# The attention output product: one head at a time over 64 partitions, in two PSUM banks, in place of head pairs with a zero-padded matrix

## The chip, the core and the metric

The program runs on one core of one Trainium2 chip. The metric is device time in microseconds, from the launch to the last write. The engines are TensorE (PE, with its weight loads shown apart as PEld), VectorE (DVE), ScalarE (ACT), GpSimd (POOL) and SyncE (SP), which here only issues transfers. SBUF and PSUM have 128 partitions; PSUM has 8 banks of 512 fp32 values per partition. A matmul holds one operand in the array (the stationary one, loaded beforehand, at most 128 partitions by 128 columns) and streams the other one past it; the columns of the stationary operand become the partitions of the result.

## The reference, cut to what matters

```python
# q, k, v: (4 batches, 8 heads, 576 tokens, 64)
kv  = einsum('bhsd,bhse->bhde', k, v)          # a 64 x 64 matrix for each batch and head
out = einsum('bhsd,bhde->bhse', q, kv)         # the "o product"
rms = sqrt(mean(out * out, axis=-1) + 1e-6)    # for each token and head
x   = out / rms * g_norm                       # then (b, s, h*d): 2304 tokens x 512
h = x @ w_in                                   # 512 -> 1024
solu = h * softmax(h); ln = layernorm(solu) * g_ln
x2 = ln @ w_out                                # 1024 -> 512
result = ((x2 @ w_a) * (x2 @ w_b)) @ w_out2    # 512 -> 1536 -> 512
```

The change touches `kv` and `out` alone. The weights arrive as 64-bit floats and are narrowed on the chip.

## The kernel before, in words

**Tiles.** The 2304 tokens are 18 tiles of 128. A batch has 576 tokens, four full tiles and 64 left over; the leftovers of two batches share a tile, so tiles 8 and 17 are mixed: 64 tokens of one batch, 64 of the next. The other 16 are full.

**Two parts.** The first part runs from the start to some 300 us and takes each tile through attention, the first feed-forward layer up to the layer norm, and (two tiles at a time) `w_out`. The second part, the last product and the two that are multiplied, is not touched.

**The steps of a tile**, by the tokens that the written order uses for them, with the engine that does the work:

- `kp` (PE, `kv_product`, L334) makes the two 64 x 64 matrices of one batch and one pair of heads, the even head on partitions 0 to 63 of a PSUM tile, the odd head on 64 to 127. `kk` (DVE) or `ka` (ACT), both `kv_keep` (L347), copy them into `kvb`, in two instructions.
- `qt` (PE, L358) transposes a tile of q, all heads: of each pair of heads, the even one lands on partitions 0 to 63 and the odd one on 64 to 127. `qk` (ACT) copies that to `qT`.
- `op` (PE, `o_product`, L370) multiplies. `kvb` for a head pair is a 128 x 128 matrix with the even head's 64 x 64 block top left, the odd head's bottom right and zeros elsewhere, so one matmul over 128 partitions gives both heads. The stationary operand is `qT` of the pair (128 partitions by 128 tokens), and the 128 columns of `kvb` stream. A full tile takes 4 such matmuls, a mixed tile 8 with 64 tokens each. The operands are plain fp32, and each matmul stands as two instructions in the trace. The result of all heads is one PSUM bank, `po`.
- `os` (ACT, `o_square`, L385) squares `po`, `om` (DVE, then POOL) sums the squares per head and takes the reciprocal root in ten small POOL instructions, `ox` (DVE, `o_scale`, L400) multiplies `po` by it. `ox` is the last reader of `po`.
- `xt`, `xh`, `xl` transpose the scaled tile (PE) and split it into a high and a low part (ACT, DVE); `hp` (PE) is the product with `w_in`, 24 matmuls into two banks of its own; `hm`, `he`, `hs`, `hq`, `hn` are maximum, exponential, product, squares and norm on DVE, ACT and POOL; `lt0`, `lt1`, `lh0` to `ll1` transpose and split the result; `yp` (PE) and `yk` (ACT) are a quarter of the product with `w_out` for two tiles and its copy.

**Order.** Each engine works strictly in the order in which the program names its instructions. That order is written out by hand: `PROLOGUE` (L26) until the tile before slot 5, then the strings `SLOT` (L37, tiles up to slot 9) and `LATER` (L41) once for each tile. A token with `+2` works on the tile two ahead. B, M, E and their like narrow weights in between on ACT, DVE and POOL. In the slots `op` stands between `xt` and `yp` (`SLOT`) or between `xt` and `lt0` (`LATER`), and `ox` near the very end. The prologue has seven `op`, the slots eleven.

**PSUM.** `hp` has two banks of its own. All other results of PE in this part take one bank each out of the pool `ps_t` (L175), six banks; a bank comes free when the last reader of its tile in the written order is done, and a product that finds none free waits.

Of the kernel before, what the change touches and what calls it, by code (L numbers as in the profile page):

```python
# [8 lines left out]
F32 = mybir.dt.float32  # L9
# [4 lines left out]
AF = mybir.ActivationFunctionType  # L14
ALU = mybir.AluOpType
# [4 lines left out]
P = 128  # L20
# [80 lines left out]
def tile_attention_moe(ctx, tc, q, k, v, g_norm, w_in, w_out, g_ln, w_a, w_b, w_out2, out):  # L101
    nc = tc.nc
    B, H, S, D = q.shape
# [3 lines left out]
    NP = H // 2  # L107
# [19 lines left out]
    tiles = []  # L127
# [19 lines left out]
    def pool(name, bufs, stack=left, side="left", **kw):  # L147
        if side == "right":
            kw["side"] = "right"
        if stack is psum:  # L150
            kw["space"] = PSUM
        return stack.enter_context(tc.tile_pool(name=name, bufs=bufs, **kw))
# [11 lines left out]
    wt = pool("wt", 1, top)  # L164
# [10 lines left out]
    ps_t = pool("ps_t", 6, psum)  # L175
# [6 lines left out]

    const.tile([P, 80], F32, name="lpad")

    kvb = [wt.tile([P, NP, P], F32, name=f"kvb{n}") for n in range(3)]
    for t in kvb:
        nc.gpsimd.memset(t, 0.0)

    def rsqrt(v, n, tag, eng=nc.gpsimd):

# [110 lines left out]
    qT = {}  # L301
# [45 lines left out]
    def kv_keep(copy=nc.vector.tensor_copy):  # L347
        if kvps:
            b, hp, pk = kvps.pop(0)
            for n in range(2):  # L350
                ns = slice(n * D, (n + 1) * D)
                copy(kvb[b % 3][ns, hp, ns], pk[ns])
            ready.add((b, hp))

    ready = set()
    psum_of = {}
# [12 lines left out]

    def o_product(i):  # L370
        assert all((b, hp) in ready for b, _, _ in tiles[i] for hp in range(NP))
        po = ps_t.tile([P, NP, P], F32, tag="t", name="po").rearrange("p n (two d) -> p (n two) d", two=2)
        for hp in range(NP):
            a = 0
            for b, _, n in tiles[i]:
                nc.tensor.matmul(  # L376
                    po[a:a + n, 2 * hp:2 * hp + 2, :], qT[i][:, hp, a:a + n], kvb[b % 3][:, hp, :],
                    start=True, stop=True,
                )
                a += n  # L380
        psum_of["o", i] = po

    sqs = {}

    def o_square(i):  # L385
        sqs[i] = tx.tile([P, H, D], F32, tag="sq", name="sq", bufs=1)
        nc.scalar.activation(sqs[i], psum_of["o", i], AF.Square)

    rms = {}

# [9 lines left out]
    def o_scale(i):  # L400
        x = tx.tile([P, H, D], F32, tag="x", name="x")
        r = rms.pop(i).rearrange("p (h o) -> p h o", o=1).to_broadcast([P, H, D])
        nc.vector.tensor_tensor(out=x, in0=psum_of.pop(("o", i)), in1=r, op=ALU.mult)
        xt[i] = x.rearrange("p h d -> p (h d)")


# [582 lines left out]
    def load_gl(_):  # L989
# [5 lines left out]
        B=lambda _: begin(), BP=lambda _: begin(True), M=lambda _: mid(), MM=lambda _: mid(2),  # L995
        E=lambda _: end(), EV=lambda _: end(nc.vector),
        kp=kv_product, kk=lambda _: kv_keep(), ka=lambda _: kv_keep(nc.scalar.copy),
        qt=q_turn, qk=q_keep, op=o_product, os=o_square, om=o_rms, ox=o_scale, xt=x_turn, xh=x_hi, xl=x_lo,
        hp=h_product, hm=h_max, he=h_exp, hs=h_solu, hq=h_square, hn=h_norm,
        lt0=lambda i: l_turn(i, 0), lt1=lambda i: l_turn(i, 1),  # L1000
# [46 lines left out]
    i = NTILE - 2  # L1047
# [8 lines left out]
    i = NTILE - 1  # L1056
# [30 lines left out]
    t = p2["x2"].tile([P, 14 * TB + 3 * LINE], F32R, tag="x", name="x2")  # L1087
    t = t[:, :14 * TB].rearrange("p (h n c t) -> p h n c t", h=2, n=7, c=2)
# [5 lines left out]
    for n, (count, which) in enumerate(((1, now), (6, later), (5, now), (2, later))):  # L1094
# [3 lines left out]
        for _ in range(count):  # L1098
            part, n = which.pop(0)
# [18 lines left out]
    for j in range(1, NJ - 1):  # L1118
        n = 2 * j + 2
# [181 lines left out]
```

## Time and profile before

| what | value |
|---|---|
| median of 2 runs | 701.88 us (701.71 to 702.06) |
| the profiled execution's own time | 702.19 us |
| its span on the core | 700.1 us |
| PE, PEld busy | 665.7 us (95%), 633.0 us (90%) |
| DVE, ACT, POOL busy | 519.6 us (74%), 284.1 us (41%), 302.8 us (43%) |
| mean granted TensorE clock | 0.995 of full speed |

The profile is one execution, recorded by the hardware. A group of instructions is named by its line, its engine and what it writes and reads: `po<-kvb,qT` is the o product, `kvp<-vs,ks` the kv product, `sq<-po` the square, `x<-po,y_a` the scaling, `xtp`, `ltp`, `qtp` the three kinds of transposes, `ph<-wih,xh` and the like the product with `w_in`, `x2p` that with `w_out`. Matmuls overlap: the recorded duration of one is its time through the array, while the next one starts earlier, so the rate is read from starts. A row of several merged instructions gives the first start and the time to the last end. Clock 1.00 is full speed.

### The profile page before, as it was taken

What the parts mean: (1) busy time and instruction counts of PE and PEld (TensorE: products, weight loads), DVE (VectorE), ACT (ScalarE), POOL (GpSimd) and SP (SyncE); (2) the same over time, 40 slices, a digit from 0 to 9 for tenths busy, and PEclk for the clock granted to TensorE, in tenths of its full rate; (3) what the DMA queues carried; (4) which work ended last, traced back from release to release, by engine and by line L of the source; (5) the groups of instructions that cost most, each with busy time, mean ns of one, the idle gap of its engine ahead of it and who ended that gap; (6) DMA issues with size and microseconds to landing.
All of it is one profiled execution on the core that took longest, in us unless ns stands there. A gap on an engine that the chain in (4) does not pass through costs nothing.

```text
span 700.1 us, 12578 instructions
## 1 busy us (share of the span) xinstructions
PE 665.7 (95%) x4710; PEld 633.0 (90%) x4710; DVE 519.6 (74%) x930; ACT 284.1 (41%) x491; POOL 302.8 (43%) x446
## 2 busy tenths in 40 slices
PE   1699999999999999999999999999999999999998
PEld 1577798999999998899999999999998899999998
DVE  3889977676688776779656867577656779987883
ACT  2558854544455346543331122212212445443431
POOL 2588776677666311113654467444672140000000
PEclk9899999999999999999999999999999999999999
DMA  9998645645542502342344336544334694654521
GB/s 248 316 248 234 184 127 156 168 127 149 178 127 76 167 16 68 106 136 81 111 149 136 118 106 187 177 136 142 112 95 129 221 313 139 190 146 130 150 76 61
DMA packets 107132, 103.84 MB, mean 148 GB/s; under 512 B 25280, under 2 KB 94400, under 8 KB 107072
## 3 DMA queue, kind: packets, MB, share of 16 engines
q1 hardware_dynamic: 101024, 94.40, 46.3%
q10 hardware_dynamic: 6048, 8.65, 3.7%
q8 instruction: 37, 0.61, 0.4%
q14 instruction: 23, 0.19, 0.1%
HBM read 71.05 MB, written 31.98 MB: 147 GB/s over the span
## 4 chain that ended last, share of the span: by engine, by line
PE 76%; DVE 9%; issue 5%; POOL 4%; DMA 3%; ACT 1%; SPq 1%; DVEq 0%; ACTq 0%; POOLq 0%
PE pw L710 26%; PE pq L881 18%; PE x2p L527 5%; PE x2p L525 5%; PE x2p L526 5%; PE ph L438 4%; PE ph L440 4%; PE ph L439 4%; PE ltp L495 2%; PE po L376 2%; DMA vs<-in_v_dram 1%; POOL a L751 1%; DMA wo<-w2d 1%; DMA gw<-gd 1%; PE xtp L413 1%
## 5 line engine op out<-in xcount | busy, mean ns | idle before, releaser
L751 POOL TENSOR_TENSOR a<-b,a 128x384 f32<-128x384 f32 x53 | 63.3, 1208 | 127.2 <-DVE b L740 126.2
L710 PE MATMUL pw<-xh,wh 128*128 128x384 f32 x336 | 114.3, 340 | 2.6 <-DVE b L761 1.6
L710 PE MATMUL pw<-xh,wl 128*128 128x384 f32 x336 | 112.7, 335 | 0.0
L710 PE MATMUL pw<-xl,wh 128*128 128x384 f32 x336 | 112.6, 335 | 0.0
L710 PE MATMUL pw<-x,wh 128*128 128x384 f32 x336 | 85.8, 336 | 0.9 <-DVE b L740 0.6
L525 PE MATMUL x2p<-lh,woh 128*128 128x256 f32 x288 | 82.6, 287 | 0.3 <-ACT lh L505 0.2
L526 PE MATMUL x2p<-ll,woh 128*128 128x256 f32 x288 | 80.6, 280 | 0.8 <-DVE ll L508 0.8
L527 PE MATMUL x2p<-lh,wol 128*128 128x256 f32 x288 | 80.6, 280 | 0.5 <-DVE wol L50 0.5
L710 PEld LDWEIGHTS pw<-xh,wh 128*128 128x128 f32 x336 | 63.1, 188 | 7.1 <-DVE b L761 2.3
L710 PEld LDWEIGHTS pw<-xl,wh 128*128 128x128 f32 x336 | 63.1, 188 | 0.0
L710 PEld LDWEIGHTS pw<-xh,wl 128*128 128x128 f32 x336 | 63.1, 188 | 0.0
L710 PEld LDWEIGHTS pw<-x,wh 128*128 128x128 f32 x336 | 60.5, 188 | 1.8 <-DVE b L740 0.9
L438 PE MATMUL ph<-wih,xh 128*128 128x512 f32 x144 | 56.9, 395 | 0.8 <-DVE so L461 0.8
L881 PE MATMUL pq<-wo,gh 128*128 128x256 f32 x336 | 57.7, 276 | 0.0
L440 PE MATMUL ph<-wih,xl 128*128 128x512 f32 x144 | 56.3, 391 | 1.2 <-DVE xl L423 1.2
L439 PE MATMUL ph<-wil,xh 128*128 128x512 f32 x144 | 56.3, 391 | 0.4 <-DVE wil L50 0.4
L710 PE MATMUL pw<-x,wl 128*128 128x384 f32 x168 | 56.2, 335 | 0.0
L527 PEld LDWEIGHTS x2p<-lh,wol 128*128 128x128 f32 x288 | 54.6, 190 | 0.9 <-DVE wol L50 0.9
L526 PEld LDWEIGHTS x2p<-ll,woh 128*128 128x128 f32 x288 | 54.2, 188 | 1.2 <-DVE ll L508 1.2
L525 PEld LDWEIGHTS x2p<-lh,woh 128*128 128x128 f32 x288 | 54.2, 188 | 0.9 <-ACT lh L505 0.5
L881 PE MATMUL pq<-wo,gw 128*128 128x256 f32 x450 | 53.1, 276 | 0.0
L67 POOL TENSOR_SCALAR nu<-nu 128x512 f32<-128x512 f32 x23 | 44.7, 1955 | 17.1 <-ACT nu L62 16.1
(158 smaller groups left out, 1536.0 us busy)
## 6 DMA issues: line engine op xcount, KB each, us to landing
gd<-a SPq DMA_DIRECT2D x72, 192.0 KB, 2.0
ring<-in_moe_w_out_dram SPq DMA_DIRECT2D x20, 512.0 KB, 5.4
gl<-gd SPq DMA_DIRECT2D x14, 384.0 KB, 3.5
gw<-gd SPq DMA_DIRECT2D x12, 384.0 KB, 3.2
ring<-in_moe_w_in_dram SPq DMA_DIRECT2D x8, 512.0 KB, 7.3
qs<-in_q_dram SPq DMA_DIRECT2D x16, 256.0 KB, 6.5
x2d<-x2s ACTq DMA_DIRECT2D x32, 128.0 KB, 1.8
st<-in_moe_w_a_dram SPq DMA_DIRECT2D x8, 512.0 KB, 4.3
```

The costliest lines, as they stand in the source:

```text
L67: eng.tensor_scalar(out=u, in0=u, scalar1=2.0 ** -15, scalar2=122879.9921875, op0=ALU.max, op1=ALU.min)
L376: nc.tensor.matmul(po[a:a + n, 2 * hp:2 * hp + 2, :], qT[i][:, hp, a:a + n], kvb[b % 3][:, hp, :], start=True, stop=True,)
L438: nc.tensor.matmul(ph[:, n, :], xh[:, c, :], wh, start=(c == 0), stop=False)
L439: nc.tensor.matmul(ph[:, n, :], xh[:, c, :], wl, start=False, stop=False)
L440: nc.tensor.matmul(ph[:, n, :], xl[:, c, :], wh, start=False, stop=(c == NK - 1))
L495: nc.tensor.transpose(pt[:, m, :], hs_[i]["so"][:, f * P:(f + 1) * P], ident)
L525: nc.tensor.matmul(pa, wh[:, cs], lh[:, f, :], start=(f == 0), stop=False)
L526: nc.tensor.matmul(pa, wh[:, cs], ll[:, f, :], start=False, stop=False)
L527: nc.tensor.matmul(pa, wl[:, cs], lh[:, f, :], start=False, stop=(f == NF1 - 1))
L710: nc.tensor.matmul(out, wt_[:, wn, c], xt_[xn][:, c], start=first and c == n == 0, stop=c == 1 and n == 2, skip_group_check=not first,)
L751: eng.tensor_tensor(out=a[n], in0=by, in1=a[n], op=ALU.mult)
L881: nc.tensor.matmul(ps, xt_[:, c], wt_[:, c], start=first and c == n == 0, stop=c == NJ - 1 and n == 2, skip_group_check=not first,)
```

## The change

`kvb` loses its zeros: it holds 64 columns for each head pair, the even head on partitions 0 to 63 and the odd one on 64 to 127, so the three memsets go and `kv_keep` copies a pair in one instruction. `o_product` issues one matmul for each head, over its 64 partitions: the stationary operand is 64 partitions by 128 tokens (64 in a mixed tile), and 64 columns stream. The even heads' results go to one PSUM bank and the odd heads' to another, head pair by head pair in turn, so a full tile has 8 matmuls in place of 4 and a mixed tile 16 in place of 8, and each takes two banks of `ps_t` and not one. `o_square` and `o_scale` do the two banks one after the other, 256 elements each, and write every second group of 64 of the same tiles as before. The order of the tokens is unchanged.

```diff
@@ -182,9 +182,7 @@
 
     const.tile([P, 80], F32, name="lpad")
 
-    kvb = [wt.tile([P, NP, P], F32, name=f"kvb{n}") for n in range(3)]
-    for t in kvb:
-        nc.gpsimd.memset(t, 0.0)
+    kvb = [wt.tile([P, NP, D], F32, name=f"kvb{n}") for n in range(3)]
 
     def rsqrt(v, n, tag, eng=nc.gpsimd):
 
@@ -347,9 +345,7 @@
     def kv_keep(copy=nc.vector.tensor_copy):
         if kvps:
             b, hp, pk = kvps.pop(0)
-            for n in range(2):
-                ns = slice(n * D, (n + 1) * D)
-                copy(kvb[b % 3][ns, hp, ns], pk[ns])
+            copy(kvb[b % 3][:, hp], pk)
             ready.add((b, hp))
 
     ready = set()
@@ -369,22 +365,28 @@
 
     def o_product(i):
         assert all((b, hp) in ready for b, _, _ in tiles[i] for hp in range(NP))
-        po = ps_t.tile([P, NP, P], F32, tag="t", name="po").rearrange("p n (two d) -> p (n two) d", two=2)
+        po = [ps_t.tile([P, NP, P], F32, tag="t", name=f"po{n}")[:, :, :D] for n in range(2)]
         for hp in range(NP):
             a = 0
-            for b, _, n in tiles[i]:
-                nc.tensor.matmul(
-                    po[a:a + n, 2 * hp:2 * hp + 2, :], qT[i][:, hp, a:a + n], kvb[b % 3][:, hp, :],
-                    start=True, stop=True,
-                )
-                a += n
+            for b, _, rows in tiles[i]:
+                for n in range(2):
+                    ns = slice(n * D, (n + 1) * D)
+                    nc.tensor.matmul(
+                        po[n][a:a + rows, hp, :], qT[i][ns, hp, a:a + rows], kvb[b % 3][ns, hp, :],
+                        start=True, stop=True,
+                    )
+                a += rows
         psum_of["o", i] = po
+
+    def of_head(t, n):
+        return t.rearrange("p (hp two) d -> p hp two d", two=2)[:, :, n]
 
     sqs = {}
 
     def o_square(i):
         sqs[i] = tx.tile([P, H, D], F32, tag="sq", name="sq", bufs=1)
-        nc.scalar.activation(sqs[i], psum_of["o", i], AF.Square)
+        for n, po in enumerate(psum_of["o", i]):
+            nc.scalar.activation(of_head(sqs[i], n), po, AF.Square)
 
     rms = {}
 
@@ -400,7 +402,8 @@
     def o_scale(i):
         x = tx.tile([P, H, D], F32, tag="x", name="x")
         r = rms.pop(i).rearrange("p (h o) -> p h o", o=1).to_broadcast([P, H, D])
-        nc.vector.tensor_tensor(out=x, in0=psum_of.pop(("o", i)), in1=r, op=ALU.mult)
+        for n, po in enumerate(psum_of.pop(("o", i))):
+            nc.vector.tensor_tensor(out=of_head(x, n), in0=po, in1=of_head(r, n), op=ALU.mult)
         xt[i] = x.rearrange("p h d -> p (h d)")
 
 
```

## Rows read from the trace of the kernel before

**Rows 1.** The page: the span, and the chain that ended last by engine

```profile
span 700.1 us, 12578 instructions
...
PE 76%; DVE 9%; issue 5%; POOL 4%; DMA 3%; ACT 1%; SPq 1%; DVEq 0%; ACTq 0%; POOLq 0%
```

**Rows 2.** Stretch 96.2 to 258.6: busy us of PE, PEld, DVE, ACT, POOL; then L376

```profile
96.20:258.60 162.40, 162.09 (x1207) 147.92 (x1206) 119.30 (x261) 75.59 (x144) 99.43 (x192) 1.00 0.48 138
...
96.20:258.60 162.40, 11.70 (x104) 10.45 (x104) 1.00 0.48 138
```

**Rows 3.** PE in order of time, 147.6 to 149.0: start, us, line, shape, count

```profile
147.98 1.06 PE L376 MATMUL po<-kvb,qT 128*128 128x128 f32 x8
```

**Rows 4.** PE in order of time, 118.4 to 119.9, around a mixed tile

```profile
118.21 0.49 PE L413 MATMUL xtp<-ident,x 128*128 128x128 f32 x3
118.63 1.09 PE L376 MATMUL po<-kvb,qT 128*64 128x128 f32 x16
119.66 0.39 PE L525 MATMUL x2p<-lh,woh 128*128 128x256 f32 x1
119.88 0.28 PE L526 MATMUL x2p<-ll,woh 128*128 128x256 f32 x1
```

**Rows 5.** PE in order of time, 151.5 to 152.6, a kv product

```profile
151.71 0.80 PE L342 MATMUL kvp<-vs,ks 128*64 128x64 f32 x20
```

**Rows 6.** Weight loads (PEld) in order of time, at 24.4 and at 118.6

```profile
24.36 0.30 PEld L376 LDWEIGHTS po<-kvb,qT 128*128 128x128 f32 x2 [1.30 <-ACT qT L367]
...
118.63 0.20 PEld L376 LDWEIGHTS po<-kvb,qT 128*64 128x64 f32 x4 [0.17 <-ACT lh L505]
```

**Rows 7.** Groups by line and shape on ACT: count, busy us, mean ns

```profile
L535 ACT COPY x2s<-x2p 128x256 f32<-128x256 f32 x32 | 12.0, 374 | 20.0 <-PE x2p L527 16.9 <-ACT x2s L535 1.8 <-DMA x2d<-x2s 1.1
...
L387 ACT ACTIVATE sq<-po 128x512 f32<-128x512 f32 x18 | 11.0, 610 | 0.8 <-PE po L376 0.7
```

**Rows 8.** Groups by line and shape on DVE

```profile
L740 DVE TENSOR_TENSOR b<-pw,b 128x384 f32<-128x384 f32 x54 | 29.6, 552 | 12.3 <-PE pw L710 12.3
...
L403 DVE TENSOR_TENSOR x<-po,y_a 128x512 f32<-128x512 f32 x18 | 12.4, 688 | 6.1 <-POOL y_a L203 6.0
...
L352 DVE COPY kvb<-kvp 64x64 f32<-64x64 f32 x16 | 3.5, 220 | 0.3
```

**Rows 9.** The chain that ended last, 0 to 97 us: start, us, what

```profile
22.15 0.61 ACT sq L387
...
28.46 0.69 DVE x L403
...
73.95 0.60 DVE x L403
```

**Rows 10.** PE in order of time, 61 to 98, the late prologue

```profile
62.11 1.04 PE L362 MATMUL qtp<-ident,qs 128*128 128x128 f32 x8
63.07 0.80 PE L342 MATMUL kvp<-vs,ks 128*64 128x64 f32 x20
64.56 1.13 PE L376 MATMUL po<-kvb,qT 128*128 128x128 f32 x8 [0.68 <-DVE ll L508]
65.61 0.80 PE L342 MATMUL kvp<-vs,ks 128*64 128x64 f32 x20
66.98 0.47 PE L438 MATMUL ph<-wih,xh 128*128 128x512 f32 x1 [0.56 <-DVE so L461]
...
87.54 0.29 PE L525 MATMUL x2p<-lh,woh 128*128 128x256 f32 x1
```

**Rows 11.** DVE in order of time, 61 to 98

```profile
64.33 0.74 DVE L423 SCALAR_TENSOR_TENSOR xl<-xtp,gn,xh 128x512 fp32r<-128x512 f32 x1
...
67.90 0.68 DVE L508 TENSOR_TENSOR ll<-ltp,lh 128x512 fp32r<-128x512 f32 x1
...
72.73 1.23 DVE L446 TENSOR_REDUCE nm<-ph 128x1 f32<-128x1024 f32 x1
...
89.64 0.69 DVE L403 TENSOR_TENSOR x<-po,y_a 128x512 f32<-128x512 f32 x1 [1.25 <-POOL y_a L203]
```

## Prediction before the change was run

> **What bounds the kernel now.** I read the page first: one core, and PE on 76% of the chain that ended last [rows 1]. The idle time of the other engines is therefore worth little by itself. Then I cut the time into stretches. From 96.2 to 258.6 us, PE is busy in 162.09 of 162.40 us at the full 2.4 GHz clock, and the o product (L376) takes 11.70 of them in 104 instructions [rows 2]: nine tiles of 8 and the two mixed tiles of 16, since one fp32 matmul is two instructions on PE. In that stretch each nanosecond that the o product gains or loses on PE goes to the end. Before it, up to 96 us, the seven other o products lie in the written-out prologue, where the chain runs mostly over DVE and POOL; there the question is what PE is kept waiting for. After 258.6 us nothing of the change runs.
>
> **Term 1, the o product on PE.** A full tile now issues 8 instructions; the last starts 1.06 - 0.275 us (one instruction) after the first, so the step is 0.112 us and the block 0.895 us [rows 3]. The change issues 16 instructions: each streams 64 columns and not 128, over 64 partitions, with 128 tokens still stationary. So streaming halves per instruction and the number of instructions doubles. The gain depends on two neighbours on different row halves of the array running side by side, and on the weight loads.
>
> *Streaming.* The trace has neighbours on different column halves: 20 instructions of 64 columns with 64 stationary columns last 0.80 us with the final 0.22, so a pair of them takes 0.058 us [rows 5], and they do run in pairs. No row has row halves. *Weight loads.* Two loads of 128 columns start 0.30 - 0.19 = 0.11 us apart before any matmul holds them up; of four loads of 64 columns, two and two at once, the second pair starts 0.06 us after the first (0.20 less one load of 0.135) [rows 6]. Both have 128 rows, and the time follows the columns. The new stationary tile keeps its 128 columns and halves its rows, so I bound its load by 0.058 and 0.11 us and take 0.11, the row with the same columns. With two halves side by side, eight pairs go at 0.108 us, plus 0.055 for the last matmul: the step stays what it was, set by the loads and not by the streaming.
>
> The Trainium skill speaks to both ends. "TensorE: Matmul & The Clock Gate", section LDWEIGHTS, says that the load takes the time of its columns whatever the rows, which speaks against a gain here; "TensorEngine Tiling (Array Packing)", section Theoretical Speedup, gives up to 2x for a contraction of 64 or less. By the first the block stays at some 0.9 us of steps, by the second it falls to half. No run so far shows 64 rows.
>
> *Changing the shape of the array.* The mixed tile shows what a block of another shape costs at its ends: the last transpose starts at 118.21 + 0.49 - 0.275 = 118.43, the first o matmul at 118.63, 0.09 more than a step of 0.109; behind the last o matmul (118.63 + 1.09 - 0.27 = 119.45) the next starts at 119.66, again 0.09 too late, and its successor at 119.88, 0.11 late since a weight load is no longer hidden [rows 4]. A full tile pays none of this today and will pay 0.29 us. New block: 8 x 0.108 + 0.055 + 0.29 = 1.21, that is +0.32 us, nine times: **+2.9**. A mixed tile now takes 0.09 + 0.82 + 0.11 + 0.20 = 1.22 us; it becomes 32 instructions on four quarters, 8 steps of 0.058 + 0.055 + 0.29 = 0.81 if all four run at once, 1.1 if they are held up by issue; I take 0.87, twice: **-0.7**. Term 1: **+2.2 us**.
>
> **Terms 2 and 3, PSUM banks.** The pool `ps_t` has six banks, and the o tile now holds two from `op` to `ox`. In the steady slots that fits: by the written order at most six are held at once, and the seventh comes after the transposed l tiles are given back. In the prologue it doesn't, at two places that I found by listing, in PE's order, which tiles still have a reader to come.
>
> *Term 2.* At 65.61 PE starts a kv product [rows 10]. Held at that moment: one transposed l tile, two q transposes (62.11), the kv product of 63.07, and the o tile of 64.56, now twice: six. So it waits for the first reader in the written order, `ll` on DVE at 67.90, which ends at 68.58 [rows 11]. The o tile itself also waits for its second bank until `xl` (64.33 + 0.74) is done [rows 11], half a microsecond late, and with its squares in two this pushes `ll` to 68.9. Behind the waiting kv product (0.73 us, and 0.15 for its shape) stands the h product, which then starts at 69.85 and not at 66.98 [rows 10]. Its maximum follows directly at 72.73 [rows 11], and the chain goes on from there: **+2.9 us**; at least 2.3 if `ll` isn't pushed, and nothing if banks are not held as I list them.
>
> *Term 3.* At 87.54 PE starts the second y product [rows 10]. Held: both o banks of tile 6, the first y product (its copy stands behind all four), one x and two l transposes: six. The next bank is given by `ox` at 89.64 [rows 11], now two instructions, the first done at 90.06. So the product starts at 90.1: **+2.6 us**, and PE is the bound from there on. The second o bank covers the third product. Bounds: 0, and 3.0 if the bank given is the second one.
>
> **Term 4, the two halves on ACT and DVE.** `ox` on 512 elements takes 0.688, an addition out of PSUM on 384 takes 0.552, so 256 take 0.416 by the same slope, and two 0.83: +0.14 [rows 8]. Six of them lie on the chain of the prologue, from 28.46 to 73.95 [rows 9]: +0.84. The square takes 0.610 on 512, a copy of 256 out of PSUM 0.374 [rows 7]: two are 0.75 at least, so +0.14 to +0.22; it is on the chain once, at 22.15 [rows 9]. Sum **+1.0 us**. In the steady stretch both are hidden by PE. One copy in place of two of 0.22 in `kv_keep` [rows 8] saves time that I count as nothing, at most 0.4 us on the chain; the three memsets that go lie in the first microseconds, while the core waits for its first data. No DMA is added or moved, and no queue is passed.
>
> **Sum.** 2.2 + 2.9 + 2.6 + 1.0 = 8.7 us on the profiled execution of 702.19 us: 710.9. That execution is 0.3 above the median of the runs, 701.88, so I forecast **710.6 us**, 1.2% slower.
>
> **Rivals.**
> (a) *The loads of the two row halves take turns.* The same 0.108 us then holds for each matmul, not for each pair: 16 x 0.108 + 0.055 + 0.29 = 2.07 us a full tile (+1.18, nine times 10.6), and 32 loads at 0.055 + 0.29 = 2.05 a mixed one (+0.83, twice 1.7). Term 1 becomes +12.3, the time 720.7, slower by over 2%; it decides so from some 0.085 us a matmul on. For it: nothing in the trace shows two loads at once on different rows. Against: loads on different columns go two at once [rows 6]. Chance 0.15.
> (b) *The bank waits don't bite,* because they fall into time that DVE has to spend anyway: terms 2 and 3 vanish, 705.1 us. For it: DVE is the bound just before both places. Against: both readers are late for reasons that a waiting PE doesn't change. Chance 0.2.
> (c) *The new loads are short,* 0.058 a pair: 8 x 0.058 + 0.11 + 0.29 = 0.86 us a tile, term 1 about -1.0, the time 707.4, and 701.9 if (b) holds too. Chance 0.15. This is where the factor in the Trainium skill, "TensorEngine Tiling (Array Packing)", section Theoretical Speedup, would lead.
> That the halves would not be packed at all is (a).
>
> **Numbers.** My forecast has a chance of 0.45, (a) 0.15, (b) 0.2, (c) 0.15, other 0.05. Range 702.5 to 719: the low end takes in (b) and most of (c), the high end my own with worse banks; (a)'s centre is left out. 2%, 14 us, is about what a measurement can tell from no change. Faster by that much 0.01 (the whole of L376 in the steady stretch is 11.7 us), within it 0.79, slower 0.20.
>
> **What would show it.** The profile after should show the full block at about 16 instructions in 0.9 us with gaps of 0.09 on both sides; a kv product near 69 and a y product near 90 that wait for DVE; the steady slot longer by 0.3 us. A step of 0.108 per instruction speaks for (a), a block under 0.6 us for (c), no new waits before 96 us for (b). I would be wrong altogether if the steady slots also ran out of banks: each of those has an `ox` at its very end.

## The result, and the profile after

The changed kernel takes **709.64 us** (two runs, 707.67 and 711.61) against 701.88: the ratio is **1.0117, 95% interval 1.0085 to 1.0149**. It is slower by 7.8 us, and the forecast was 710.6. The profile after is the execution of 707.67 us. From the page, the span, the busy times and the shares of the chain of waits by engine:

```profile
span 705.9 us, 12925 instructions
...
PE 671.6 (95%) x4870; PEld 636.4 (90%) x4870; DVE 517.1 (73%) x940; ACT 282.6 (40%) x501; POOL 300.1 (43%) x443
...
PE 77%; DVE 8%; DMA 4%; POOL 4%; issue 3%; ACT 2%; SPq 1%; ACTq 0%; DVEq 0%; POOLq 0%
```

PE is still 77% of the chain [rows 1]: no other engine became the bound. Lines have moved: the kv product is L340, the o product L374, its square L389, the scaling L406, the h product L441 to L443, the y product L528 to L530.

**The steady stretch and the late prologue.** The view of stretches gives busy us of PE, PEld, DVE, ACT and POOL, the granted clock, the DMA share and GB/s; the second line is the o product alone.

```profile
102.00:273.00 171.00, 170.44 (x1367) 154.38 (x1366) 121.26 (x271) 80.21 (x163) 98.34 (x193) 1.00 0.46 132
...
102.00:273.00 171.00, 11.37 (x208) 9.85 (x208) 1.00 0.46 132
...
66.00:72.80 6.80, 4.51 (x34) 3.76 (x33) 6.42 (x16) 6.41 (x14) 5.14 (x15) 0.50 0.75 156
```

PE is as full as before at full clock [rows 2], and 208 instructions of the o product take 11.37 us of busy time where 104 took 11.70. So half the streaming has bought nothing. The last line is new: in 66.0 to 72.8 us the granted clock was 0.50, that is 1.2 and not 2.4 GHz. Before, no such stretch lies between 60 and 100 us. Earlier in the prologue both profiles have some, the one after for longer (18.2 to 21.6 and 25.0 to 38.7 us, against 19.1 to 22.5 and 29.3 to 32.8), but that cost nothing: at 63 us the same PE operations start at the same times in both.

**One full and one mixed tile on PE**, in order of time (start, us, operation, shape, count):

```profile
154.29 0.60 PE L416 MATMUL xtp<-ident,x 128*128 128x128 f32 x4
154.82 1.11 PE L374 MATMUL po<-kvb,qT 64*128 64x64 f32 x16
155.86 0.39 PE L528 MATMUL x2p<-lh,woh 128*128 128x256 f32 x1
156.08 0.28 PE L529 MATMUL x2p<-ll,woh 128*128 128x256 f32 x1
...
125.43 0.69 PE L374 MATMUL po<-kvb,qT 64*64 64x64 f32 x32
126.05 0.38 PE L528 MATMUL x2p<-lh,woh 128*128 128x256 f32 x1
```

The same place in the kernel before, around the o product of [rows 3]:

```profile
147.54 0.60 PE L413 MATMUL xtp<-ident,x 128*128 128x128 f32 x4
...
148.79 0.37 PE L525 MATMUL x2p<-lh,woh 128*128 128x256 f32 x1
148.99 0.28 PE L526 MATMUL x2p<-ll,woh 128*128 128x256 f32 x1
```

From the first o matmul to the next operation a full tile takes 155.86 - 154.82 = 1.04 us; before it was 0.81 (147.98 to 148.79), so this part grew by 0.23. Ahead of it, the last transpose starts 0.20 us ahead of the first o matmul (154.29 + 0.60 - 0.27 = 154.62); in the kernel before it was 0.11 (147.87), so 0.09 more. Behind it, the successor comes 0.22 us later and not 0.20: 0.02 more. Within the block an even and an odd head start 0.007 us apart, and the pairs follow at 0.112 us, the very step that a single matmul of 128 partitions had. A mixed tile, on four quarters, is done in 0.69 us where it took 1.09 [rows 4].

The weight loads (PEld), the first four of a full and of a mixed tile:

```profile
154.82 0.30 PEld L374 LDWEIGHTS po<-kvb,qT 64*128 64x128 f32 x4 [0.17 <-ACT lh L508]
...
125.43 0.15 PEld L374 LDWEIGHTS po<-kvb,qT 64*64 64x64 f32 x4 [0.17 <-ACT lh L508]
```

In 0.30 us go four loads of 64 rows and 128 columns where two of 128 by 128 went [rows 6]: those of the two row halves run side by side, and a pair takes what one took. On quarters all four run in 0.15.

The slot from tile to tile, read on the chain of waits at the l transposes (start, us), after and then before:

```profile
138.68 0.87 PE ltp L498 x8
...
153.58 0.87 PE ltp L498 x8
```

```profile
132.27 0.87 PE ltp L495 x8
...
146.83 0.87 PE ltp L495 x8
```

14.90 against 14.56: each slot with a full tile is 0.34 us longer, the sum of those three.

**The two places in the prologue, and a third**, PE in order of time, with idle time before an operation and what ended it in brackets:

```profile
65.44 1.44 PE L374 MATMUL po<-kvb,qT 64*128 64x64 f32 x14 [0.26 <-DVE xl L426]
...
69.17 1.33 PE L340 MATMUL kvp<-vs,ks 128*64 128x64 f32 x20 [2.29 <-DVE va L481]
70.43 0.80 PE L441 MATMUL ph<-wih,xh 128*128 128x512 f32 x1
71.02 0.63 PE L442 MATMUL ph<-wil,xh 128*128 128x512 f32 x1
...
82.31 0.63 PE L416 MATMUL xtp<-ident,x 128*128 128x128 f32 x4 [0.78 <-DVE ll L511]
...
91.64 0.28 PE L530 MATMUL x2p<-lh,wol 128*128 128x256 f32 x1
93.86 0.36 PE L528 MATMUL x2p<-lh,woh 128*128 128x256 f32 x1 [1.94 <-DVE x L406]
```

And DVE, in order of time:

```profile
64.55 0.74 DVE L426 SCALAR_TENSOR_TENSOR xl<-xtp,gn,xh 128x512 fp32r<-128x512 f32 x1
...
68.33 0.68 DVE L511 TENSOR_TENSOR ll<-ltp,lh 128x512 fp32r<-128x512 f32 x1
...
77.32 1.22 DVE L449 TENSOR_REDUCE nm<-ph 128x1 f32<-128x1024 f32 x1 [4.28 <-PE ph L443]
78.46 0.74 DVE L406 TENSOR_TENSOR x<-po,y_a 128x256 f32<-128x256 f32 x2
...
81.48 0.69 DVE L511 TENSOR_TENSOR ll<-ltp,lh 128x512 fp32r<-128x512 f32 x1
...
93.29 0.76 DVE L406 TENSOR_TENSOR x<-po,y_a 128x256 f32<-128x256 f32 x2 [1.23 <-POOL y_a L201]
```

The kv product stood still for 2.29 us. The bracket names `va`, a small instruction just behind `ll` on DVE; `ll` ended at 69.01, and the product started at 69.17, 3.56 us later than before. The h product is 3.45 us late [rows 10], and then its instructions take 0.63 us each, at half clock, so its maximum is 4.6 us late, at 77.32 [rows 11]. The second y product waited 1.94 us for the scaling `x`, and started 0.15 us after the first of its two halves ended (93.71), before the second did. The third place is the transposition of the scaled tile 5 at 82.31: its operand `x` was done at 79.20, yet PE stood still for 0.78 us until `ll` on DVE ended (82.17), so what it lacked was again a bank. It started 5.3 us later than before (77.05), where it did not wait. All ten profiles of kernels with two banks have this wait, of 0.3 to 1.2 us, and none of the three with one.

**The halves on ACT and DVE**, groups by line (count, busy us, mean ns):

```profile
L389 ACT ACTIVATE sq<-po 128x256 f32<-128x256 f32 x36 | 12.1, 398 | 1.2 <-PE po L374 1.2
...
L406 DVE TENSOR_TENSOR x<-po,y_a 128x256 f32<-128x256 f32 x36 | 13.5, 414 | 6.3 <-POOL y_a L201 6.3
```

One half of the scaling lasts 0.414 us, as estimated, but two in a row are done in 0.74 to 0.76 (above), against 0.688 in one [rows 8].

**Where the 5.8 us between the two spans lie**, by the starts of the same PE operations before and after: nothing at 63 us, +3.45 at the h product, +5.3 at 82 us, +4.3 just before the second y product (slack that the stretch has), +6.3 at it, +6.0 at 100 us, +8.4 at 240 us, +7.5 at the last y product, and +5.8 at the end. So the first part lost some 8 us, and the second, which the change doesn't touch, was about 2 shorter in this execution. Of that second part, the view of waits (engine, line, waited for: us in total, times, longest) has in the changed kernel, and in the kernel before:

```profile
PE pw L713 <- DVE b L764: 0.5, 1, 0.5
```

```profile
PE pw L710 <- DVE b L761: 1.6, 2, 1.3
```

PE waited 1.1 us less at this line. The change is not needed for it: from the last transposition of the first part (271 us in the kernel before) to the end, the profile before is longer than all twelve others, by 0.7 to 3.4 us, also those where only the squares and the scaling are halved (experiment 2, 1.1 us) or only the order is moved (experiment 6, 1.5 us). What makes it vary is not shown.

### The profile page after: what moved, and what is told of

Same layout as the page of the kernel before. It is cut to its first block, busy times and chain, and to the rows that moved or that the text cites. A ratio compares the mean times of both kernels' runs of the same rounds, so it can differ in the third digit from the quotient of the medians.

```text
span 705.9 us, 12925 instructions
## 1 busy us (share of the span) xinstructions
PE 671.6 (95%) x4870; PEld 636.4 (90%) x4870; DVE 517.1 (73%) x940; ACT 282.6 (40%) x501; POOL 300.1 (43%) x443
## 4 chain that ended last, share of the span: by engine, by line
PE 77%; DVE 8%; DMA 4%; POOL 4%; issue 3%; ACT 2%; SPq 1%; ACTq 0%; DVEq 0%; POOLq 0%
PE pw L713 30%; PE pq L884 18%; PE x2p L528 4%; PE x2p L529 4%; PE x2p L530 4%; PE ph L441 4%; PE ph L443 4%; PE ph L442 3%; PE ltp L498 2%; PE po L374 2%; DMA vs<-in_v_dram 1%; PE kvp L340 1%; POOL t_a L201 1%; DMA x2d<-x2s 1%; DVE so L464 1%
## 5 line engine op out<-in xcount | busy, mean ns | idle before, releaser
L528 PE MATMUL x2p<-lh,woh 128*128 128x256 f32 x288 | 82.3, 286 | 2.6 <-DVE x L406 1.9
L530 PE MATMUL x2p<-lh,wol 128*128 128x256 f32 x288 | 80.0, 278 | 0.0
L441 PE MATMUL ph<-wih,xh 128*128 128x512 f32 x144 | 58.3, 405 | 0.4 <-DVE so L464 0.4
L443 PE MATMUL ph<-wih,xl 128*128 128x512 f32 x144 | 57.5, 399 | 0.2 <-DVE xl L426 0.2
L528 PEld LDWEIGHTS x2p<-lh,woh 128*128 128x128 f32 x288 | 54.1, 188 | 3.8 <-issue 2.1
L530 PEld LDWEIGHTS x2p<-lh,wol 128*128 128x128 f32 x288 | 54.4, 189 | 0.0
```

Of the source, the lines that this page charges most:

```text
L441: nc.tensor.matmul(ph[:, n, :], xh[:, c, :], wh, start=(c == 0), stop=False)
L443: nc.tensor.matmul(ph[:, n, :], xl[:, c, :], wh, start=False, stop=(c == NK - 1))
L528: nc.tensor.matmul(pa, wh[:, cs], lh[:, f, :], start=(f == 0), stop=False)
L530: nc.tensor.matmul(pa, wl[:, cs], lh[:, f, :], start=False, stop=(f == NF1 - 1))
```

## The experiments

My theory: slower by the sum of three things, the o block on PE (2.2 us), a kv product and a y product that wait for a bank (2.9 and 2.6), and two halves on ACT and DVE (1.0). The rival after the result: half the clock in the late prologue, which no term had. All ratios are to runs of the kernel before on the same chip in the same session.

### 1. Two banks alone

The kernel before, with its zero-padded matmuls and head pairs 0 and 1 in one bank, 2 and 3 in another:

```diff
-        po = ps_t.tile([P, NP, P], F32, tag="t", name="po").rearrange("p n (two d) -> p (n two) d", two=2)
+        po = [ps_t.tile([P, NP, P], F32, tag="t", name=f"po{n}").rearrange("p n (two d) -> p (n two) d", two=2)[:, :4] for n in range(2)]
...
-                    po[a:a + n, 2 * hp:2 * hp + 2, :], qT[i][:, hp, a:a + n], kvb[b % 3][:, hp, :],
+                    po[hp // 2][a:a + n, hp % 2 * 2:hp % 2 * 2 + 2, :], qT[i][:, hp, a:a + n], kvb[b % 3][:, hp, :],
...
-        nc.scalar.activation(sqs[i], psum_of["o", i], AF.Square)
+        for n, po in enumerate(psum_of["o", i]):
+            nc.scalar.activation(sqs[i][:, 4 * n:4 * n + 4], po, AF.Square)
```

> The kernel before, with its zero-padded 128-row matmuls, but the results of head pairs 0 and 1 in one PSUM bank and of pairs 2 and 3 in another, squares and scaling in two halves. Theory (bank waits in the prologue plus the halves are most of the loss): a kv product that waits until about 69 us, the h product behind it at half the clock, a y product near 93 us, and 707 to 708.5 us. Rival (the loss sits in the matmul shape): no new wait before 96 us, 702 to 703.5 us.

Measured: 707.81 us, ratio 1.0073 (1.0049 to 1.0097), +5.9 us. PE in order of time:

```profile
68.80 1.34 PE L342 MATMUL kvp<-vs,ks 128*64 128x64 f32 x20 [2.75 <-DVE va L481]
70.07 0.80 PE L441 MATMUL ph<-wih,xh 128*128 128x512 f32 x1
...
94.38 0.36 PE L528 MATMUL x2p<-lh,woh 128*128 128x256 f32 x1 [1.93 <-DVE x L406]
```

Both waits are there with the old matmuls, and so is the half clock (0.50 from 67.5 to 74.3). The loss of this profile lies before 96 us (+8.0 there, +7.9 at 259 us). The second bank, with the half clock that comes with it, carries three quarters of the loss.

### 2. Two halves, one bank

The kernel before, with the square and the scaling done for even and odd heads apart:

```diff
-        nc.scalar.activation(sqs[i], psum_of["o", i], AF.Square)
+        for n in range(2):
+            nc.scalar.activation(of_head(sqs[i], n), of_head(psum_of["o", i], n), AF.Square)
...
+        po = psum_of.pop(("o", i))
+        for n in range(2):
+            nc.vector.tensor_tensor(out=of_head(x, n), in0=of_head(po, n), in1=of_head(r, n), op=ALU.mult)
```

> The kernel before with one bank and its old matmuls; only the square and the scaling are done in two instructions of 256 elements, for even and odd heads. Theory: 1.0 us more (term 4), 702.9 us, within 0.5. Rival (the split on ACT and DVE delays the chain more than its own time and carries the loss): 705 us or more.

Measured: 701.26 us, ratio 0.9981 (0.9965 to 0.9997). Nothing is lost; the expectation fell. DVE in order of time:

```profile
74.55 0.74 DVE L409 TENSOR_TENSOR x<-po,y_a 128x256 f32<-128x256 f32 x2
```

Two halves take 0.05 us more than one whole, not 0.14.

### 3. The waits taken out of the order, first try

The changed kernel; the h product goes ahead of the kv product, and the first y product with its copy goes ahead by six tokens:

```diff
-hs+2 kp hp+3 os+5 hq+2 om+5 ll1 hn+2 xt+4 LQ E qk+6 MM LK ka qk+7 B E kp lt0+1 lt1+1 ka xh+4 hm+3
+hs+2 hp+3 kp os+5 hq+2 om+5 ll1 hn+2 xt+4 LQ E qk+6 MM LK ka qk+7 B E kp lt0+1 lt1+1 ka xh+4 hm+3
...
-EV hp+4 BP hq+3 lh0+2 hm+4 he+4 ox+6 hn+3 hs+4 ll1+2 xh+5 yp yp yp yp xl+5 ll0+2 lt0+3 lt1+3 hq+4
+EV hp+4 BP hq+3 lh0+2 yp yk hm+4 he+4 ox+6 hn+3 hs+4 ll1+2 xh+5 yp yp yp xl+5 ll0+2 lt0+3 lt1+3 hq+4
```

> The changed kernel with two moves in the written order of the prologue: the h product of tile 3 goes ahead of the kv product that waits for a bank, and the first y product is copied out at once, so that its bank serves the second. Theory: both waits and the half clock go, some 3.5 + 1.8 + 1.9 us; 702.5 to 704.5 us remain, for the longer slots. Rival (the waits fall in time that DVE or POOL fill anyway): 708 us or more.

Measured: 705.58 us, ratio 1.0055 (1.0036 to 1.0074), +3.7 us, 1 us beyond what I expected. The first wait went, and in the profiled execution the half clock with it (1.00 in 60 to 100 us); that execution, of 703.92 us, is the fastest of ten, and in four of the others the mean clock over the whole run was 0.977 to 0.983. The waits of PE in that stretch show why the rest stayed:

```profile
PE x2p L528 <- DVE x L406: 1.9, 1, 1.9
```

The bank of the first y product was free early (copied out by 89.02 us, while the second product started at 90.56), but the second product takes the next one in the pool's turn, and that was still the o tile's. So which bank comes free matters, not only how many.

### 4. Only the kv product moved

The first of those two moves alone:

```diff
-hs+2 kp hp+3 os+5 hq+2 om+5 ll1 hn+2 xt+4 LQ E qk+6 MM LK ka qk+7 B E kp lt0+1 lt1+1 ka xh+4 hm+3
+hs+2 hp+3 kp os+5 hq+2 om+5 ll1 hn+2 xt+4 LQ E qk+6 MM LK ka qk+7 B E kp lt0+1 lt1+1 ka xh+4 hm+3
```

> The changed kernel with one move: the h product of tile 3 ahead of the kv product that waits for a bank. Theory (that wait costs 3.5 us and the half clock behind it 1.8): 704 to 706 us. Rival (only the wait itself counts, or DVE takes it up again): 706.5 us or more.

Measured: 706.91 us, ratio 1.0078 (1.0055 to 1.0102), in the rival's range. The wait is gone, yet the stretch of half clock is there (view of stretches):

```profile
66.80:73.60 6.80, 6.11 (x15) 4.79 (x15) 6.22 (x16) 5.94 (x12) 5.50 (x14) 0.50 0.67 141
```

PE is busy for 6.11 of these 6.80 us, at 1.2 GHz. The half clock is therefore not tied to the kv product's wait alone. It also took back what the move had won: the h product started only 0.6 us later than in the kernel before, but the transposition behind it 4.2 us later, against 4.6 in the changed kernel; 0.8 of that is the kv product, which now stands between them, and some 2.8 the clock.

### 5. Both waits taken out

The kv product moved as before, and `ll1+2`, the reader that gives back the bank, put ahead of `hp+4`:

```diff
-EV hp+4 BP hq+3 lh0+2 hm+4 he+4 ox+6 hn+3 hs+4 ll1+2 xh+5 yp yp yp yp xl+5 ll0+2 lt0+3 lt1+3 hq+4
+EV ll1+2 hp+4 BP hq+3 lh0+2 hm+4 he+4 ox+6 hn+3 hs+4 xh+5 yp yp yp yp xl+5 ll0+2 lt0+3 lt1+3 hq+4
```

> The move of the kv product and, for the second wait, the low part of the second half of tile 2 on DVE ahead of the maximum of tile 4, so that a transposed tile's bank is free when the second y product starts (the earlier mend of that wait left it at 1.9 us). Theory: no bank wait over 0.5 us in the late prologue, 703 to 704.5 us, what the longer slots and small waits leave. Rival (the second wait falls in time that is lost anyway): as with the kv product alone, 705 us or more.

Measured: 703.73 us, ratio 1.0036 (1.0022 to 1.005), +2.2 us. PE's longest waits in 60 to 100 us:

```profile
PE po L374 <- DVE ll L511: 0.9, 1, 0.9
...
PE xtp L416 <- DVE ll L511: 0.5, 1, 0.5
PE x2p L528 <- DVE ll L511: 0.4, 1, 0.4
```

No kv product waits for a bank any longer, nor does the second y product, and 5.5 of the 7.7 us are back. Waits for `ll` remain, and that of the o product is over the 0.5 us that I had set (0.7 in the kernel before [rows 10]). The 2.2 us left have the size of term 1, but the profile does not divide that way: 1.8 us are lost by 96 us, with the clock at 0.50 from 68.5 to 71.9, and 2.2 more over the steady stretch by 259 us; the rest of that execution was 3.4 us shorter than in the profile before.

### 6. The kernel before with these two moves

> The kernel before with the two moves in the written order and nothing else. Theory (the moves only remove bank waits, which this kernel doesn't have): 701 to 702.5 us, no change. Rival (the lead of the quarters kernel comes from the moves): 699 to 700 us.

Measured: 700.76 us, ratio 1.0000 (0.9984 to 1.0015): just under my range, and no change by the ratio. The moves help only a kernel that holds two banks; experiment 5 reads the banks and not a better order.

### 7. The o product on quarters

The changed kernel, with each full tile's 128 tokens as two stationary tiles of 64:

```diff
-                for n in range(2):
-                    ns = slice(n * D, (n + 1) * D)
...
+                for a in range(a, a + rows, D):
+                    for n in range(2):
+                        ns = slice(n * D, (n + 1) * D)
+                        nc.tensor.matmul(
+                            po[n][a:a + D, hp, :], qT[i][ns, hp, a:a + D], kvb[b % 3][ns, hp, :],
```

> The changed kernel with each full tile's product in two halves of 64 tokens: stationary 64 partitions by 64 tokens, four neighbours on four quarters of the array, 32 instructions a tile as in the mixed tiles. Theory (the step of a pair is set by the load of 128 stationary columns): steps of 0.058 us, a block shorter by 8 x (0.112 - 0.058) = 0.43 us less half a load, nine times: 3 to 4 us gained, 706 us. Rival (the ends of the block or the streaming set it): 709 to 710 us.

Measured: 706.01 us, ratio 1.0046 (1.0028 to 1.0064), as expected. PE in order of time:

```profile
155.05 0.69 PE L375 MATMUL po<-kvb,qT 64*64 64x64 f32 x32
155.68 0.39 PE L529 MATMUL x2p<-lh,woh 128*128 128x256 f32 x1
```

Twice as many instructions take 0.63 us to the next operation, not 1.04: the columns of the load set the step.

### 8. Even heads first, then odd

The changed kernel, with the loop over even and odd outside the one over pairs, so that neighbours use the same row half:

```diff
-        for hp in range(NP):
+        for n, hp in ((n, hp) for n in range(2) for hp in range(NP)):
```

> The changed kernel with the even heads of a tile first and the odd ones after, so that neighbours lie on the same row half and not side by side. Theory (a pair costs one load of 128 columns because the two row halves load and stream at the same time): the step of 0.112 us then holds for each matmul, a full tile's block of 16 takes about 1.8 us and not 1.1, a slot is 0.8 us longer, and the time 717 to 719 us. Rival (the row halves do not run side by side, the order does not matter): 709 to 710 us, block unchanged.

Measured: one run, 713.74 us, beside a median of 701.49 for the kernel before. PE in order of time, a whole block, and then its first six instructions:

```profile
156.55 1.60 PE L374 MATMUL po<-kvb,qT 64*128 64x64 f32 x16
158.08 0.38 PE L528 MATMUL x2p<-lh,woh 128*128 128x256 f32 x1
...
156.55 0.82 PE L374 MATMUL po<-kvb,qT 64*128 64x64 f32 x6
```

The block is 1.53 us long to the next operation, not 1.04. That the turn of halves packs them is confirmed; the size came out at half, since five even matmuls start alone at 0.11 us apart, and from 157.05 the odd ones run beside the last three even ones.

### 9. Filler ahead of the waiting kv product

The changed kernel with ten 512-column matmuls into the banks of the h product, which overwrites them, issued before the kv product, to keep PE at work through the wait:

```diff
-hs+2 kp hp+3 os+5 hq+2 om+5 ll1 hn+2 xt+4 LQ E qk+6 MM LK ka qk+7 B E kp lt0+1 lt1+1 ka xh+4 hm+3
+hs+2 hd+3 kp hp+3 os+5 hq+2 om+5 ll1 hn+2 xt+4 LQ E qk+6 MM LK ka qk+7 B E kp lt0+1 lt1+1 ka xh+4
...
+    def h_filler(i):
+        ph = early_ph[i] = ps_h.tile([P, 2, HALF], F32, tag="h", name="ph")
+        for k in range(10):
+            nc.tensor.matmul(ph[:, k % 2, :], xT[i][0][:, 0, :], wi[0, 0][0], start=True, stop=True)
```

> The changed kernel with ten extra matmuls of 512 columns between the o product of tile 5 and the waiting kv product, into the banks of the h product of tile 3, which overwrites them; PE waits for the same bank but works meanwhile. Theory (behind the wait the h product runs at half the clock because PE stood still): the kv product stays at about 69 us, the h matmuls behind it go at 0.23 us and not 0.43, 1 to 2 us less than the changed kernel beside it. Rival (the fall of the clock is older than the wait): half clock remains until some 73 us, no gain.

Measured: 709.9 us, ratio 1.0111 (1.0082 to 1.014): no gain. PE in order of time:

```profile
67.01 4.06 PE L451 MATMUL ph<-wih,xh 128*128 128x512 f32 x10 [0.69 <-DVE so L471]
71.00 0.80 PE L340 MATMUL kvp<-vs,ks 128*64 128x64 f32 x20
71.73 0.50 PE L441 MATMUL ph<-wih,xh 128*128 128x512 f32 x1
72.07 0.39 PE L442 MATMUL ph<-wil,xh 128*128 128x512 f32 x1
```

The filler itself ran at half clock (0.50 from 66.9 to 70.3 us), 0.4 us each, and ended 1.8 us after the kv product would have started; the h product behind it then ran at full clock. So the clock had already fallen when the filler began. In the profile after, too, the stretch at 0.50 begins at 66.0 us and the wait only at 66.88, where the o block ends (65.44 + 1.44): the fall is older than the wait, and this run is no measure of what the half clock costs.

### 10. The changed kernel again

> The changed kernel once more, in more executions: 707 to 711.5 us, median near 709, since stretches at half the clock in the prologue come and go (in the profiles so far 3 to 20 us of them before 100 us). If the clock has no part in the spread, its executions should lie within 1 us.

Measured: 709.38 us (708.85 to 710.46), ratio 1.0116 (1.0099 to 1.0132). Its profiled execution, of 710.46 us, shows a further stretch of half clock, at the y products (view of stretches):

```profile
95.70:99.10 3.40, 3.40 (x18) 3.40 (x18) 3.33 (x8) 1.24 (x2) 2.73 (x9) 0.50 0.02 5
```

The profiles of experiments 1, 4, 7 and 9 have such a second stretch too, at 94 to 98 us. The four executions lie 1.6 us apart, but at nearly the same mean clock (0.992 to 0.993), so this run does not show that the clock makes the spread. My 3 to 20 us before 100 us was also too narrow: the profiles up to then go from none (experiments 3 and 11) to some 30 (experiment 4).

### 11. Quarters, and both waits taken out

The edits of experiments 5 and 7 together.

> Both moves and full tiles in quarters of 64 by 64. Theory: the longer slots go too, 3 to 3.5 us less than with both moves alone, 700 to 701.5 us, just under the kernel before. Rival (quarters gained by shortening the prologue alone): 703 us or more.

Measured: **698.76 us (698.29 to 701.65), ratio 0.9968 (0.9956 to 0.9981)**: faster than both kernels, by 0.3% against before. The late prologue in the view of stretches, and two l transposes of neighbouring slots on PE:

```profile
60.00:100.00 40.00, 36.01 (x331) 31.48 (x330) 36.14 (x72) 26.79 (x53) 31.14 (x64) 1.00 0.60 155
```

```profile
132.04 1.03 PE L499 MATMUL ltp<-ident,so 128*128 128x128 f32 x8
...
146.53 1.03 PE L499 MATMUL ltp<-ident,so 128*128 128x128 f32 x8
```

The slot is 14.49 us, 0.07 under the kernel before, and there is no half clock in this execution. It gained 5.0 us over experiment 5 and not the 3 to 3.5 expected. In the two profiles 3.5 us of it lie in the steady stretch, as expected, and 1.6 before 96 us, where experiment 5's has 0.50 from 68.5 to 71.9. Against the profile before, the first part gained 1.1 us; the rest of the 3.5 us between the two spans lies behind it, where the change has no part.

## Why the prediction was right, point by point

**Term 1, +2.2 us: right.** The pairs go at 0.112 us (0.108 taken), 0.11 us of it for the load of 128 columns; a full tile costs 0.34 us more with its ends (0.32 taken); two mixed tiles cost less, 0.4 us each (0.35 taken). Over the steady stretch, both mixed tiles included, the delay grows from 5.9 to 8.2 us by 259 us, 2.3 us, 0.44 of which is one wait for POOL at 123.5 us; in the changed kernel's second profile it grows by 1.6, in those of experiments 4 and 5 by 1.5 and 2.2. The choice that carried it was to let the row with the same columns set the load, against the row with the same size of matmul. The Trainium skill, "TensorE: Matmul & The Clock Gate", section LDWEIGHTS, states that the columns count and not the rows; the trace agrees, 0.11 us for 64 rows and 128 columns. Its "TensorEngine Tiling (Array Packing)", section Theoretical Speedup, names up to 2x for a contraction of 64; with 128 stationary columns no run here shows any, and with 64 the block falls from 0.81 us in the kernel before to 0.63.

**Term 2, +2.9 us: the mechanism right, the consequence too small.** (Its own parts, 68.9 + 0.73 + 0.15, make 69.78 and not 69.85.) The kv product waited for the bank that `ll` gives back, at 69.17 (68.9 foreseen), and the h product came 3.45 us late (2.9). What the term lacked is the clock: the h product, behind the wait of 2.29 us, ran at 1.2 GHz until 72.8 us, and the delay grew by 1.1 us, to 4.6. The listing of banks also missed a third place: the transposition at 82.31 waited 0.78 us for `ll`, and the delay grew to 5.3. Moving the kv product gives no sure measure of the term, since the half clock stayed without the wait (experiment 4).

**Term 3, +2.6 us: right in place, mis-sized.** The y product waited for the first half of the scaling, as taken. Between the last y product before it and itself, 0.22 us passed before (87.32 to 87.54) and 2.22 after: +2.0. The delays from the first place had left some slack here: the last y product before it came 4.3 us later than in the kernel before (91.64 for 87.32), the scaling only 3.65 (93.29 for 89.64). The prediction added the two as if there were no slack.

**Term 4, +1.0 us: wrong.** It added the mean time of two halves, but on DVE the second half starts before the first is over (0.76 for two of 0.414), and two halves in the kernel before lost nothing (experiment 2). The step that failed is "two 0.83: +0.14", as the price of a pair and as a loss on the chain six times over.

**The sum** was 8.7 us, and the medians differ by 7.8, but not term by term. In the profile the first part lost 8.4 by 240 us: 8.7 - 1.6 (terms 3 and 4) + 0.8 (terms 1 and 2, which came to 2.4 up to there and 3.45) + 1.1 (half clock) + 0.7 (the third place) - 1.3 (slack, 1.0 ahead of the second y product and 0.3 after it). Errors of either sign cancelled, so it is partly luck that the time came out within 1 us of the forecast. What holds is the mechanism: waits for banks in the late prologue and a longer o block.

**The rivals.** (a), loads that take turns, is refuted by the pairs at 0.112 us; experiment 8 shows what a kernel pays in which they partly do, 713.7. (b), waits that don't bite, is refuted by experiments 1 and 5. (c), short loads, is refuted for 128 columns; it holds with 64, where the step is 0.058 for a group of four. Half the clock was no rival of mine and should have been one.

**Open:** what sets off the half clock. It came with the kv wait removed (experiment 4), stayed away with the same move in experiments 3 and 11, and began before the wait in the profile after. It varies between executions: in the late prologue the changed kernel's second profile has two such stretches, its first one. No run keeps the waits and takes away the half clock alone, so how much of the second bank's 5.9 us is the clock is open too, and so is why the part behind the first varies by up to 3.4 us between profiles.

## What to carry to other kernels

Halving the partitions of a matmul gains nothing while the stationary operand keeps its columns and the load sets the step; cut both, and change the shape of the array seldom, since each block pays for it at both ends. Count PSUM banks at each place of the written order before giving a tile a second one: here the bank cost 5.9 us, with the half clock that came along, more than the matmuls, and moving two tokens won back 5.5. A version with quarters and those two moves then beat the kernel before, by 0.3%.

## What the runs showed of the hardware that I had not expected

- Two DVE instructions of 256 elements per partition out of PSUM, 0.414 us each, are done in 0.74 to 0.76 us together: a sum of means overstates a pair.
- With even heads ahead of odd ones, the odd matmuls did not wait for the last even ones: a whole block took 1.53 us where 16 steps of 0.112 would be 1.8.
- The granted clock fell to 0.50 somewhere in the late prologue in eight of the ten profiles of kernels with two banks (the changed one twice, experiments 1, 4, 5, 7, 8 and 9; not 3 and 11), and in none of the three with one bank (the kernel before, experiments 2 and 6).
